# Three score rounds of the second batch put into one burst of a planned attention and feed-forward kernel

## The chip, the cores and the metric

The kernel runs on one core of a Trainium2 chip. The metric is the time of one execution in device microseconds (us); several executions are timed and the median is given. One execution was also recorded by the hardware profiler. Its engines are called PE (TensorE, matmuls), PEld (TensorE's weight loads), DVE (VectorE), ACT (ScalarE), POOL (GpSimd) and SP (SyncE, which here only issues transfers).

## The reference

Eight batches of twelve heads, with 448 positions and 64 elements per head. The attention has a squared ReLU in the place of a softmax, and its output goes straight into a feed-forward block with the same squared ReLU.

```
scores = scale * q @ k.T                  # per batch and head, 448 x 448
attn   = max(scores, 0) ** 2 / S          # S = 448
x      = (attn @ v), heads side by side   # 3584 x 768
g      = max(x @ w_in, 0) ** 2            # 3584 x 2048
out    = g @ w_out                        # 3584 x 768, float32
```

## The kernel before, in words

**Units and rounds.** A unit is four heads of one batch, so there are three units to a batch and 24 in all. The 448 positions are cut into seven blocks of 64. A round is one unit and one key block: `scores` (L525) multiplies four heads at once on TensorE as four 64x64 tiles, four matmuls that fill two PSUM banks. Rounds are numbered through: 0 to 20 belong to the first batch, 21 to 41 to the second. `squared` then empties each bank twice: `rel` = ReLU of the bank by DVE (L541) or ACT (L544), and `at` = its square by ACT (L548) or POOL (L551). When the seven rounds of a unit are squared, `av` (L591) multiplies them with v (28 matmuls in 64x64 tiles), and ACT or DVE (L611, L613) copies the result into `xt`.

**Dense work.** With a batch's `xt` complete, 16 groups of six matmuls (L653) make `g`; ACT squares the bank (L642) and DVE masks it (L637). The second product is done by a Strassen scheme: seven products of eight matmuls (L873) in place of eight. Its sums of `g` are made by DVE (`comb`, L852), its combinations of `w_out` also by DVE (`wt`, L839), and its results are put together by ACT and DVE (L793, L795, L885) and stored by SP (L749).

**Loads.** Units 0 to 5 of q and k are turned on TensorE (L463) and copied out by ACT or DVE (L466); from unit 6 on POOL casts them (L443) and SP issues a transposing transfer (L479). POOL issues the loads of v (L492), of the early q and k (L409), of `w_in` (L499) and of `w_out` (L504). The first batch is a special stream (L702, L715, L729, L732 make the first columns of `g`; L1023 are filler matmuls that the plan puts where TensorE would be idle early on).

**What sets the order.** Nothing is issued as it is written. Every operation is added to a `Plan` with a cost, its dependencies, its buffers and a due time; for matmul groups the due time is a running sum of their costs, `plan.now`. `Plan.run` then plays the plan through with sixteen pairs of rules (how long TensorE stays idle before a filler, and when POOL may take a square) and up to ten guesses of when loads land, keeps the pair whose end is earliest, and emits the instructions in the order of their planned starts. Which engine takes a `rel` or a square, which buffer is used, and the order on every queue come out of this.

**Bursts.** From the second batch on, `bursts()` gives groups of rounds. For each group the loop at L1122 adds the loads and turns that are due by then, adds the scores of its rounds, links them (`glue`: TensorE prefers the next linked piece, and waits up to 0.45 us of plan time for it), puts the `av` of the finished unit behind the second round where the group names one, and then calls `run_some`, which adds dense work in proportion to the length of the group. The first groups are listed by hand in `FIRST` (L1000); later units have groups of four and three rounds.

Of the kernel before, what the change touches and what calls it, by code (L numbers as in the profile page):

```python
# [300 lines left out]
def kernel(  # L301
# [654 lines left out]
    def push_dense(b):  # L956
# [36 lines left out]
        if b == 0 and PLAIN0:  # L993
# [3 lines left out]
    EARLY = 6  # L997
    PLAIN0 = False
    NPE = 6
    FIRST = (((21,), None), ((22, 23), None), ((24, 25), None), ((26, 27), None), ((28, 29), None),  # L1000
             (range(30, 34), 3), ((34, 35), None), ((36, 37), None), (range(38, 42), 4))
    STEPS = (0, 1, 2, 3), (4, 5, 6)
    ROUNDS = NUN * TJ
# [2 lines left out]
    def bursts():  # L1006

        for rs, n in FIRST:
            yield list(rs), n
# [187 lines left out]
```

## Time and profile before

| | |
|---|---|
| median of 6 runs | 379.53 us (378.63 to 380.4) |
| the profiled execution | 378.72 us, of which the span is 376.9 us |
| granted TensorE clock in it | 0.999 |
| PE busy | 366.5 us, 3277 matmuls |
| DVE, ACT, POOL busy | 272.7, 269.3, 221.0 us |
| moved by DMA | 51.36 MB |

The span runs from the first to the last recorded instruction; 1.82 us of the execution lie outside it. Busy times of PE and PEld overlap. A releaser in the profile is what ended an engine's idle time, and the chain is followed back from the last instruction to whatever released each step.

### The profile page before, as it was taken

What the parts mean: (1) busy time and instruction counts of PE and PEld (TensorE: products, weight loads), DVE (VectorE), ACT (ScalarE), POOL (GpSimd) and SP (SyncE); (2) the same over time, 40 slices, a digit from 0 to 9 for tenths busy, and PEclk for the clock granted to TensorE, in tenths of its full rate; (3) what the DMA queues carried; (4) which work ended last, traced back from release to release, by engine and by line L of the source; (5) the groups of instructions that cost most, each with busy time, mean ns of one, the idle gap of its engine ahead of it and who ended that gap; (6) DMA issues with size and microseconds to landing.
All of it is one profiled execution on the core that took longest, in us unless ns stands there. A gap on an engine that the chain in (4) does not pass through costs nothing.

```text
span 376.9 us, 8786 instructions
## 1 busy us (share of the span) xinstructions
PE 366.5 (97%) x3277; PEld 196.6 (52%) x3277; DVE 272.7 (72%) x472; ACT 269.3 (71%) x587; POOL 221.0 (59%) x271
## 2 busy tenths in 40 slices
PE   7799999999999999999999999999999999999995
PEld 3446555444455445545555555545555555555663
DVE  2996899968967777677977666868777687366631
ACT  5998998869966898688767678677777675243221
POOL 7999975768766777566486567856575333000100
PEclk9999999999999999999999999999999999999999
DMA  8999998497598683971588873774643002210243
GB/s 180 197 208 203 204 232 227 134 170 241 120 197 205 179 183 58 220 164 26 149 135 197 199 173 72 190 167 92 152 81 92 3 12 52 55 30 0 64 104 84
DMA packets 70218, 51.36 MB, mean 136 GB/s; under 512 B 36896, under 2 KB 70176, under 8 KB 70176
## 3 DMA queue, kind: packets, MB, share of 16 engines
q1 hardware_dynamic: 52384, 35.86, 37.9%
q0 software_dynamic: 16928, 14.09, 25.2%
q10 hardware_dynamic: 864, 0.85, 0.7%
q8 instruction: 25, 0.41, 0.4%
q14 instruction: 17, 0.14, 0.1%
HBM read 45.61 MB, written 11.01 MB: 150 GB/s over the span
## 4 chain that ended last, share of the span: by engine, by line
PE 90%; POOL 3%; ACT 2%; DMA 2%; DVE 1%; issue 1%; ACTq 0%; POOLq 0%; DVEq 0%
PE mm L653 38%; PE mm L873 34%; PE mm L525 9%; PE mm L591 8%; DMA g<-in_k_dram 2%; ACT at L548 1%; POOL w L499 1%; POOL comb L551 1%; PE mm L463 1%; DVE rel L541 1%; PE mm L702 1%; POOL vs L492 1%; ACT rel L544 0%; ACT part L793 0%; POOL g L409 0%
## 5 line engine op out<-in xcount | busy, mean ns | idle before, releaser
L551 POOL TENSOR_TENSOR at<-rel 128x448 f16<-128x448 f32 (+1 forms) x148 | 133.9, 928 | 69.1 <-DVE rel L541 51.4
L653 PE MATMUL mm<-xt,w 128*128 128x448 f16 (+1 forms) x768 | 147.8, 346 | 0.0
L637 DVE SCALAR_TENSOR_TENSOR g<-mm,g 128x448 f16<-128x448 f32 (+1 forms) x128 | 77.0, 605 | 46.4 <-ACT g L642 46.1
L653 PEld LDWEIGHTS <-w 128*128 128x128 f16 x768 | 73.1, 98 | 67.9 <-issue 7.4
L642 ACT ACTIVATE g<-mm 128x448 f16<-128x448 f32 (+1 forms) x128 | 69.6, 545 | 49.7 <-PE mm L653 49.4
L541 DVE TENSOR_SCALAR rel<-mm 128x448 f32<-128x448 f32 (+3 forms) x172 | 95.0, 594 | 11.8 <-PE mm L525 10.4
L548 ACT ACTIVATE at<-rel 128x448 f16<-128x448 f32 (+1 forms) x188 | 98.9, 593 | 0.3 <-DVE rel L541 0.3
L544 ACT ACTIVATE rel<-mm 128x448 f32<-128x448 f32 (+2 forms) x176 | 84.9, 557 | 4.6 <-PE mm L525 4.6
L873 PEld LDWEIGHTS <-comb 128*128 128x128 f16 x448 | 42.1, 98 | 33.4 <-issue 5.9
L525 PE MATMUL mm<-qkt,qkt 64*64 64x448 f16 (+2 forms) x756 | 49.6, 336 | 0.9 <-DVE rel L541 0.4
L885 DVE SCALAR_TENSOR_TENSOR part<-mm,part 128x384 f32<-128x384 f32 x56 | 30.5, 554 | 24.8 <-ACT part L793 13.3
L793 ACT ACTIVATE part<-mm 128x384 f32<-128x384 f32 x42 | 21.1, 505 | 35.4 <-PE mm L873 34.6
L443 POOL CAST blk<-raw 128x896 f16<-128x896 f32 x36 | 33.3, 930 | 20.2 <-DVE wt L839 6.5
L873 PE MATMUL mm<-w,comb 128*128 128x384 f16 x224 | 39.8, 327 | 0.0
L873 PE MATMUL mm<-wt,comb 128*128 128x384 f16 x224 | 39.6, 326 | 0.0
L873 PEld LDWEIGHTS <-g 128*128 128x128 f16 x288 | 27.7, 98 | 20.6 <-issue 2.5
L591 PE MATMUL mm<-at,vs 64*64 64x448 f16 (+1 forms) x672 | 35.2, 343 | 0.2
L873 PE MATMUL mm<-w,g 128*128 128x384 f16 x192 | 33.9, 326 | 0.3 <-DVE rel L541 0.3
L525 PEld LDWEIGHTS <-qkt 64*64 64x64 f16 x756 | 18.9, 105 | 24.2 <-issue 19.1
L492 POOL DMA_DIRECT2D vs<-in_v_dram x48 | 29.9, 632 | 1.8 <-DMA g<-in_k_dram 1.1
L774 POOL COPY rest<-g 128x1024 f16<-128x1024 f16 x8 | 8.4, 1050 | 36.0 <-DVE comb L852 35.3
L591 PEld LDWEIGHTS <-vs 64*64 64x64 f16 x756 | 21.5, 107 | 14.9 <-issue 3.8
(59 smaller groups left out, 197.2 us busy)
## 6 DMA issues: line engine op xcount, KB each, us to landing
out_dram<-part SPq DMA_DIRECT2D x108, 96.0 KB, 2.3
raw<-in_k_dram SPq DMA_DIRECT2D x18, 448.0 KB, 4.3
raw<-in_q_dram SPq DMA_DIRECT2D x18, 448.0 KB, 5.5
vs<-in_v_dram POOLq DMA_DIRECT2D x48, 112.0 KB, 5.1
w<-in_moe_w_in_dram POOLq DMA_DIRECT2D x4, 768.0 KB, 12.1
w<-in_moe_w_out_dram POOLq DMA_DIRECT2D x4, 768.0 KB, 13.5
g<-in_k_dram POOLq DMA_DIRECT2D x4, 224.0 KB, 10.8
g<-in_q_dram POOLq DMA_DIRECT2D x4, 224.0 KB, 9.8
```

Of the source, the lines that this page charges most:

```text
L443: return lambda: fn(blk.tile.rearrange("p t (f d) -> p f t d", f=2), tile_of().rearrange("p f (t d) -> p f t d", d=D))
L492: return lambda: nc.gpsimd.dma_start(out=buf.tile[64 * r:64 * r + 64], in_=src[:, u, hs])
L525: nc.tensor.matmul(sp[e].tile[64 * c:64 * c + 64, c0:c0 + w].rearrange("p (t c) -> p t c", c=TP), lhsT=kT[r, t, 64 * e:64 * e + 64], rhs=q ...
L541: dve(width, lambda: nc.vector.tensor_scalar(out=r.tile[:, 0:width], in0=bank.tile[:, 0:width], scalar1=0.0, scalar2=SK, op0=ALU.max, op1= ...
L544: act(width, lambda: nc.scalar.activation(out=r.tile[:, 0:width], in_=bank.tile[:, 0:width], func=AF.Relu, scale=SK))],
L548: act(width, lambda: nc.scalar.activation(out=dst(), in_=r.tile[:, 0:width], func=AF.Square)),
L551: lambda: nc.gpsimd.tensor_mul(dst(), r.tile[:, 0:width], r.tile[:, 0:width]))],
L591: nc.tensor.matmul(banks[f].tile[64 * e:64 * e + 64, c0:c0 + w], lhsT=vs[r, e ^ c, t * D:(t + 1) * D], rhs=a[r, e, :], start=(t == 0), sto ...
L637: nc.vector.scalar_tensor_tensor(out=dst, in0=src, scalar=0.0, in1=dst, op0=ALU.is_gt, op1=ALU.mult)
L642: nc.scalar.activation(out=dst, in_=src, func=AF.Square)
L653: nc.tensor.matmul(bank.tile[:, c0:c0 + w], lhsT=w1[f // 4][:, m, f % 4 * P:(f % 4 + 1) * P], rhs=xts[b].tile[:, m, cols], start=(m == 0), ...
L873: nc.tensor.matmul(buf.tile[:, 0:HALF], lhsT=lhs()[:, j, :], rhs=w[:, j, :], start=(first and j == 0), stop=(j == NH - 1), skip_group_chec ...
```

## The change

The first two entries of the hand-written list become one. Rounds 21, 22 and 23 are now one group, linked and followed by one call of `run_some`; before, round 21 was a group with a call of its own, and rounds 22 and 23 were the next group. Everything else in the program text is the same, but the plan is made anew, and the built program differs on every engine from its first microseconds on.

```
     EARLY = 6
     PLAIN0 = False
     NPE = 6
-    FIRST = (((21,), None), ((22, 23), None), ((24, 25), None), ((26, 27), None), ((28, 29), None),
+    FIRST = (((21, 22, 23), None), ((24, 25), None), ((26, 27), None), ((28, 29), None),
              (range(30, 34), 3), ((34, 35), None), ((36, 37), None), (range(38, 42), 4))
```

More of the change, by code (lines that the diff above doesn't have):

```diff
@@ L999 @@
     NPE = 6
-    FIRST = (((21,), None), ((22, 23), None), ((24, 25), None), ((26, 27), None), ((28, 29), None),
+    FIRST = (((21, 22, 23), None), ((24, 25), None), ((26, 27), None), ((28, 29), None),
              (range(30, 34), 3), ((34, 35), None), ((36, 37), None), (range(38, 42), 4))
```

## The prediction

> **What bounds the kernel now.** I read the page first, then the busy time by stretch, the chain of waits in order of time, TensorE's own waits, and TensorE's timeline where the edit lies. A change of 0.3%, 1.14 us, is about the least that a measurement of this kernel can tell from none.
>
> The page, TensorE's row and its 40 slices:
>
> ```profile
> PE 366.5 (97%) x3277; PEld 196.6 (52%) x3277; DVE 272.7 (72%) x472; ACT 269.3 (71%) x587; POOL 221.0 (59%) x271
> ...
> PE   7799999999999999999999999999999999999995
> ```
>
> The busy time by stretch (PE, PEld, DVE, ACT, POOL, then clock, DMA share, GB/s):
>
> ```profile
> 20.00:30.60 10.60, 9.80 (x128) 5.29 (x127) 9.61 (x23) 10.60 (x29) 10.54 (x16) 1.00 1.24 206
> 30.60:36.00 5.40, 5.40 (x96) 3.46 (x94) 2.68 (x5) 4.19 (x10) 5.40 (x9) 1.00 1.27 205
> 36.00:60.00 24.00, 24.00 (x286) 14.16 (x284) 22.30 (x42) 23.88 (x57) 20.98 (x27) 1.00 1.20 220
> 60.00:100.00 40.00, 39.66 (x334) 19.44 (x332) 34.40 (x57) 34.01 (x76) 28.52 (x34) 1.00 0.80 173
> 100.00:372.00 272.00, 271.88 (x2148) 145.48 (x2147) 190.85 (x320) 181.12 (x387) 137.51 (x159) 1.00 0.51 116
> ```
>
> Until 30.6 ACT and POOL are full and TensorE has holes; afterwards TensorE is full, with hardly a hole to the end. TensorE's waits from 36 us on are this one line:
>
> ```profile
> PE mm L873 <- DVE rel L541: 0.3, 1, 0.3
> ```
>
> TensorE's timeline around the edited rounds (21 to 23 are the 12 matmuls at 35.99):
>
> ```profile
> 29.79 0.99 PE L1023 MATMUL mm<-part 128*128 128x256 f16 x5
> 30.62 1.46 PE L702 MATMUL mm<-w,xt 128*128 128x512 f16 x6
> 32.01 0.58 PE L463 MATMUL mm<-ident,g 128*64 128x128 f16 x14
> 32.52 1.15 PE L591 MATMUL mm<-at,vs 64*64 64x320 f16 x28
> 33.60 0.58 PE L463 MATMUL mm<-ident,g 128*64 128x128 f16 x14
> 34.11 0.62 PE L729 MATMUL mm<-ident,comb 128*128 128x128 f16 x8
> 34.57 0.98 PE L653 MATMUL mm<-xt,w 128*128 128x320 f16 x6
> 35.48 0.58 PE L463 MATMUL mm<-ident,g 128*64 128x128 f16 x14
> 35.99 0.76 PE L525 MATMUL mm<-qkt,qkt 64*64 64x448 f16 x12
> ```
>
> The chain, for the price of a switch between 64x64 tiles and dense matmuls:
>
> ```profile
> 231.09 1.32 PE mm L591 x28
> 232.41 0.38 PE mm L525 x8
> 232.79 1.41 PE mm L873 x8
> 234.20 1.14 PE mm L653 x6
> ...
> 240.03 2.27 PE mm L653 x12
> 242.30 1.30 PE mm L873 x8
> 243.60 0.50 PE mm L525 x8
> ```
>
> Eight score matmuls take 0.38 us behind other tiled ones and 0.50 behind dense ones; eight of L873 take 1.30 behind dense and 1.41 behind tiled ones. A switch costs 0.12 into tiles and 0.11 out.
>
> The sum of before, from the burst at 36.06 to TensorE's end at 372.75 (336.7 us): 672 dense matmuls of 448 columns at 0.189 (127.0), 90 of 320 columns at 0.136 (12.2), 784 of L873 at 0.1625 (127.4), 588 of L525 and 588 of L591 at 0.0473 (27.8 each), 42 turns at 0.036 (1.5): 323.7. With 102 switches (11.7) that is 335.4; 1.3 us is left for all waits. Nothing much can be won behind 36 us; a loss has no such bound.
>
> **The change part by part.** At its own place the edit does nothing: the trace already has the 12 matmuls of the three rounds in one stretch. What changes is what the planner makes of it. I compared the built orders engine by engine.
>
> *Up to 30.6 us.* The four L702 groups start at 19.15, 23.09, 27.05 and 30.62, and the `w_in` parts landed at 19.1, 23.0, 26.7 and 30.5 (issue plus time to landing): the stage is paced by these landings, 3.7 to 3.9 us apart, whenever they were issued. POOL now issues the last three behind a 320-column square (0.70) in place of a 512-column one (1.06), 0.36 earlier. I take 0; the bounds are -0.36 (each landing follows its issue) and +0.3 (ACT's work to its fourth L715 is 29.1 us by its rows, 28.8 before, and ACT is full there). Two switches more lie here, under the landings.
>
> *30.6 to 37 us.* Before, L591 stood between unit 3's two turns. Now both turns come first, and the second needs its q, issued at 16.5 and landed at 32.8, while TensorE is ready at 32.5: +0.25, bounds 0 and 0.6. The burst then comes before an L653 and a turn that preceded it: 1.33 us of work exchanged, no cost. Unit 4's loads are issued up to 0.7 later; q landed at 36.2 and is needed at about 37: hidden, and 0.2 if that cover goes.
>
> *Switches.* From the burst on there are 98 in place of 102: -4 x 0.11 = -0.44. Over the whole kernel it is 116 for 118, so the bounds are -0.22 and -0.44.
>
> *Bank waits.* In the old order one PSUM bank is reused 0.5 us after its last write (the L873 at 98.97, the wait of 0.34 above). The new order spaces that one out, but in the burst near 73 us an L653 follows the 12 matmuls into the bank that their first pair filled, also 0.5 us after. ACT's `rel` (0.48) with about 0.2 to start it frees it 0.2 to 0.3 late: -0.34 + 0.3.
>
> *The `w_out` loads (L504).* POOL has 0.68 us more ahead of the first, and a 448-column square (0.93) between the first two. They landed at 44.7, 48.5, 52.3 and 58.6. DVE's first L839 stands five rows earlier, at about 50.4, and needs the second: 50.1 at the latest. Every `rel` behind it on DVE's queue, and so TensorE's banks, would wait with it. The fourth is needed by L873 at 59.7 and comes at 60.2 at the latest: +0.1, bounds 0 and 0.5.
>
> *Squares on POOL.* POOL takes 159 in place of 151 over the kernel: 8 x 0.93 = 7.4 us, under 156 us of its idle time; ACT has 8 fewer. I take 0; without that cover each costs its 0.93.
> By the Trainium skill ("SBUF — State Buffer", "SBUF: two separate sides") GpSimd and a VectorE operation with two SBUF inputs hold a shared port in turn, the loser blocked for the whole instruction, which speaks against more squares on POOL. The trace agrees: the first `wt` on DVE took 1.69 us beside a square, others 0.945. By that rule 8 squares could add 8 x 0.74 = 6 us to DVE, beside 104 us of its idle time, and the sum stays what it is.
>
> *Unit 7's transposes.* POOL casts k behind four squares now, not ahead of them; SP issues the two L479 back to back behind four stores; and TensorE wants the pair before its next L591 (1.45 us), not behind it. By adding up the rows the second L479 is issued near 75.7; time to landing ran from 2.9 to 7.1, so it lands between 78.6 and 82.8. TensorE needs it near 81.9 (83.3 before, when it landed at 79.4). I take 0.2, nearest to the 4.9 that the last one took; bounds 0 and 0.9.
>
> Sum: 0 + 0.25 - 0.44 - 0.34 + 0.3 + 0.1 + 0 + 0.2 = +0.07. On the profiled execution that is 378.72 + 0.07 = 378.8; the median of the runs stands 0.81 above it: 379.6. With all low bounds the sum is -1.1, with all high ones +2.2.
>
> **The rivals.** *Unit 7 arrives late (slower).* The mechanism above, with POOL one cast and one square further behind (1.85): a landing at 83 to 84.7 against 81.9 stops TensorE for 1 to 2.8 us, and no later stage has slack to give back. It decides from a landing behind 83. For it: 6.0 and 7.1 us are the landings of the pair issued at 77.9 and 79.3. Against it: the pair before took 2.9 and 4.9. Time: 379.4 (the forecast without its 0.2 for this) + 1.9, the middle, = 381.3.
>
> *ACT and DVE fall behind between 36 and 60 us (slower).* ACT has 0.12 us idle of 24 there, and DVE now runs both halves of its first L839 (1.25 to 1.69 each) before 58 us, where the second stood at 59.2. If one half lands in front of a `rel` for which TensorE has no other bank, TensorE waits that long, less the 0.2 or so in which a bank is not yet wanted: 379.6 + 1.3 = 380.9. Against it: the counts of `rel`, mask and L839 in that stretch are the same in both orders.
>
> *The early landings move (faster).* If the landings follow their issue, -0.36, the switches give -0.44, and the bank wait goes without another in its place, -0.34, and the exchange of turns costs nothing: -1.1 to -1.3, 378.3. For it: POOL is on the chain there. Against it: the even 3.8 us between landings.
>
> *The change doesn't do what it says.* At the place it names that holds already; had the planner made the same order, the time would be 379.5. The built orders differ, so this goes with the forecast.
>
> **How the numbers follow.** Forecast, within 1.1 us: 0.46. Unit 7 late: 0.22. ACT and DVE behind: 0.14. Early landings: 0.18. Slower by over 0.3%: most of the two slow cases (0.31) and the forecast's upper edge (0.07): 0.38. Faster: 0.18 and its lower edge 0.04: 0.22. Within: 0.40. The forecast's own range is 378.5 to 380.7; to hold 8 in 10 it goes to 378.2, into the fast case, and to 382.2, the late unit with 2.8 us.
>
> **What would show it.** Right: L702 at the same four times within 0.3; about 0.25 us before the second turn near 32.8; one short bank wait near 73 and none near 99; TensorE's chain unbroken from 37 us to the end. Wrong: a TensorE wait over 0.5 on a DMA near 82 or on DVE or ACT between 45 and 60; or the fourth L702 moved from 30.6 by more than 0.4.

## The result, and the profile after

The changed kernel takes 381.17 us in the median (21 runs, 379.43 to 382.47); the kernel before takes 379.16 us on the same chip (47 runs). The ratio is 1.0046, with a 95% interval of 1.0035 to 1.0057: slower by 1.3 to 2.2 us (the quotient of the two medians is 1.0053, inside the interval). The profiled execution took 380.41 us with a span of 378.6 (before 378.72 and 376.9), at a granted clock of 1.00. The profile of the first experiment below comes from a disturbed execution, so only that run's times are used.

The page of the changed kernel, TensorE's row and its 40 slices:

```profile
PE 369.0 (97%) x3277; PEld 197.9 (52%) x3277; DVE 271.0 (72%) x469; ACT 268.4 (71%) x582; POOL 226.2 (60%) x279
...
PE   8889999999999999999999999999999999999995
```

TensorE is still the bound, with the same 3277 matmuls, so the 1.7 us must be holes, later starts or matmuls that take longer (PE is busy 2.5 us more, 1.4 of it before 20 us: 16.43 against 15.06). Its waits from 33 us on hardly show them:

```profile
PE mm L653 <- ACT rel L544: 0.2, 1, 0.2
PE mm L525 <- DVE g L637: 0.2, 1, 0.2
```

These two stand in place of the one wait of 0.3 before. The rest is found by laying the two timelines beside each other at the same work. First TensorE's timeline of the changed kernel around the edited rounds:

```profile
31.16 1.47 PE L702 MATMUL mm<-w,xt 128*128 128x512 f16 x6
32.56 0.58 PE L463 MATMUL mm<-ident,g 128*64 128x128 f16 x14
33.07 0.28 PE L1023 MATMUL mm<-part 128*128 128x256 f16 x1
33.45 0.58 PE L463 MATMUL mm<-ident,g 128*64 128x128 f16 x14
33.96 1.15 PE L591 MATMUL mm<-at,vs 64*64 64x320 f16 x28
35.04 0.62 PE L729 MATMUL mm<-ident,comb 128*128 128x128 f16 x8
35.59 0.76 PE L525 MATMUL mm<-qkt,qkt 64*64 64x448 f16 x12
```

The fourth L702 starts at 31.16, 0.54 later than before. The filler at 33.07 covers a hole of 0.38 ahead of unit 3's second turn, whose q was issued at 16.3 and landed at 33.4. The L591 that stood at 47.18 stands at 48.10 (+0.92), so more than half of the loss is made by then. The score burst that stood at 113.37 begins at 114.36 (+0.99). The last step is near 217 us, in the chain of waits:

```profile
215.80 0.64 DVE g L637
216.44 0.02 issue
216.46 1.29 DVE comb L852
217.75 1.07 DVE rel L541 x2
218.83 0.04 issue
218.87 0.38 PE mm L525 x2
```

DVE's sum for the Strassen product (`comb`) took 1.29 us in place of 0.70, because a cast on POOL ran beside it (216.28 to 217.21):

```profile
216.28 0.93 POOL L443 CAST blk<-raw 128x896 f16<-128x896 f32 x1 [0.22 <-DMA raw<-in_q_dram]
```

That the cast is the reason is shown by the second profile of the same program, below. The two `rel` behind it freed TensorE's banks late, and the L873 that follows came 1.58 after its old place in place of 0.99. From there both timelines keep that distance to the end (374.34 against 372.75).

### The profile page after: what moved, and what is told of

Read it like the earlier page. It is cut to its first block, busy times and chain, and to the rows that moved or that the text cites. A ratio compares the mean times of both kernels' runs of the same rounds, so it can differ in the third digit from the quotient of the medians.

```text
span 378.6 us, 8785 instructions
## 1 busy us (share of the span) xinstructions
PE 369.0 (97%) x3277; PEld 197.9 (52%) x3277; DVE 271.0 (72%) x469; ACT 268.4 (71%) x582; POOL 226.2 (60%) x279
## 4 chain that ended last, share of the span: by engine, by line
PE 86%; DMA 6%; ACT 2%; POOL 2%; DVE 2%; issue 1%; ACTq 0%; POOLq 0%
PE mm L653 36%; PE mm L873 33%; PE mm L525 8%; PE mm L591 7%; DMA g<-in_q_dram 5%; DMA g<-in_k_dram 2%; POOL w L499 1%; ACT rel L544 1%; PE mm L463 1%; ACT at L548 1%; POOL comb L551 1%; ACT g L642 1%; DVE g L637 1%; DVE rel L541 0%; DVE part L885 0%
## 5 line engine op out<-in xcount | busy, mean ns | idle before, releaser
L551 POOL TENSOR_TENSOR at<-rel 128x448 f16<-128x448 f32 (+1 forms) x156 | 139.6, 918 | 71.0 <-DVE rel L541 44.1
L541 DVE TENSOR_SCALAR rel<-mm 128x448 f32<-128x448 f32 (+2 forms) x166 | 92.7, 596 | 15.8 <-PE mm L525 14.0
L548 ACT ACTIVATE at<-rel 128x448 f16<-128x448 f32 (+1 forms) x180 | 93.2, 586 | 0.8 <-DVE rel L541 0.8
L544 ACT ACTIVATE rel<-mm 128x448 f32<-128x448 f32 (+2 forms) x182 | 86.7, 546 | 6.7 <-PE mm L525 6.5
L873 PEld LDWEIGHTS <-comb 128*128 128x128 f16 x448 | 42.3, 98 | 33.1 <-issue 5.4
L525 PE MATMUL mm<-qkt,qkt 64*64 64x448 f16 (+2 forms) x756 | 50.7, 336 | 1.5 <-ACT xt L611 0.6
L885 DVE SCALAR_TENSOR_TENSOR part<-mm,part 128x384 f32<-128x384 f32 x56 | 30.5, 554 | 25.6 <-ACT part L793 15.0
L793 ACT ACTIVATE part<-mm 128x384 f32<-128x384 f32 x39 | 19.3, 495 | 36.5 <-PE mm L873 36.4
L873 PE MATMUL mm<-w,comb 128*128 128x384 f16 x224 | 39.8, 327 | 0.0
L873 PE MATMUL mm<-wt,comb 128*128 128x384 f16 x224 | 39.6, 326 | 0.0
L873 PEld LDWEIGHTS <-g 128*128 128x128 f16 x288 | 27.5, 98 | 20.9 <-issue 2.9
L591 PE MATMUL mm<-at,vs 64*64 64x448 f16 (+1 forms) x672 | 35.2, 343 | 0.1
L873 PE MATMUL mm<-w,g 128*128 128x384 f16 x192 | 34.0, 326 | 0.0
L525 PEld LDWEIGHTS <-qkt 64*64 64x64 f16 x756 | 18.7, 105 | 26.0 <-issue 20.1
L591 PEld LDWEIGHTS <-vs 64*64 64x64 f16 x756 | 21.7, 107 | 13.5 <-issue 3.1
```

Source lines behind the costliest of these rows:

```text
L525: nc.tensor.matmul(sp[e].tile[64 * c:64 * c + 64, c0:c0 + w].rearrange("p (t c) -> p t c", c=TP), lhsT=kT[r, t, 64 * e:64 * e + 64], rhs=q ...
L541: dve(width, lambda: nc.vector.tensor_scalar(out=r.tile[:, 0:width], in0=bank.tile[:, 0:width], scalar1=0.0, scalar2=SK, op0=ALU.max, op1= ...
L544: act(width, lambda: nc.scalar.activation(out=r.tile[:, 0:width], in_=bank.tile[:, 0:width], func=AF.Relu, scale=SK))],
L548: act(width, lambda: nc.scalar.activation(out=dst(), in_=r.tile[:, 0:width], func=AF.Square)),
L551: lambda: nc.gpsimd.tensor_mul(dst(), r.tile[:, 0:width], r.tile[:, 0:width]))],
L591: nc.tensor.matmul(banks[f].tile[64 * e:64 * e + 64, c0:c0 + w], lhsT=vs[r, e ^ c, t * D:(t + 1) * D], rhs=a[r, e, :], start=(t == 0), sto ...
```

## The experiments

All times are medians; each ratio is against the kernel before, run beside it on the same chip (379.0 to 379.4 us). Differences of 0.1% between two of these runs are within their intervals.

My first theory was that the planner's other pair of rules made the loss. The pair is (patience, lead): how long TensorE stays idle before a filler, and how far ahead of ACT POOL must be to take a square. The planner chose (0.45, 0.9) for the kernel before and (0.3, 1.1) for the changed one.

The end that `Plan.run` works out when a kernel is built says what the planner itself expected: 378.8 us of plan time for the old list with (0.45, 0.9), and 378.5 for the new list with (0.3, 1.1). The old list with (0.3, 1.1) comes to 380.0 and the new list with (0.45, 0.9) to 380.9. So the planner took the changed kernel for 0.3 us faster, and the first two experiments build plans that it had turned down as 1.3 and 2.1 us slower than the old one; their loss does not by itself explain that of the changed kernel.

**The new list with the rules of before.**

```
-    PATIENCE = 0.0, 0.15, 0.3, 0.45
-    LEAD = 0.7, 0.9, 1.1, 1.3
+    PATIENCE = 0.45,
+    LEAD = 0.9,
```

> The new list, with the planner held to the pair of rules that it picked for the old list (idle 0.45 us before a filler, lead 0.9; it had picked 0.3 and 1.1). The built order is that of the kernel before on every engine up to about 37 us. Theory S (the start costs: in the profiles the new kernel is 0.92 us late at the first L591 behind 36 us, 48.27 against 47.35): that L591 comes back to 47.4 within 0.3, and the ratio to before falls from 1.0046 to 1.002 or less. Rival P (the loss is the DVE and POOL collision near 217 us and others like it behind 48 us): L591 may move but the ratio stays at 1.003 or more. Rival N (the early difference is the luck of one profile): the landings of w_in differ from run to run by 0.5 whatever the order.

380.40 us, ratio 1.0043 (1.0028 to 1.0058). The rules of before do not bring the time back. Whether the L591 came back is not seen here; a later run with the same plan has it at 47.21, as before.

**The old list with the new rules** (0.3 and 1.1 put there in the same way).

> The old list, with the planner held to the pair of rules that it picked for the new one (0.3 and 1.1). The built order is that of the changed kernel up to about 33 us (up to the second turn of unit 3 and the L591 on TensorE). Theory S: the four L702 start 0.4 to 0.8 later than before (19.15, 23.09, 27.05, 30.62), the first L591 behind 36 us is 0.5 to 0.9 late, and the time is 1.002 to 1.003 of before at least. Rival P: the ratio depends on what comes behind 48 us alone. Rival N: L702 at the times of before within 0.2.

380.88 us, ratio 1.0046 (1.0029 to 1.0064). Its start is the changed kernel's, with the wait of 0.48 before the first L702 and the L591 at 47.79. But the four L702 (19.79, 23.14, 26.81 and 30.80) are not 0.4 to 0.8 late as expected: the last is 0.18 behind the kernel before. Behind that TensorE waits 0.4, 0.3 and 0.3 for banks, near 90, 100 and 183 us, where the kernel before waits 0.3 once. So the old list loses as much under the new rules as the new list does under either pair; 1.3 of its 1.6 us the planner had expected.

**Unit 3's second turn behind the L591 again.** After the planning, the turn of q is moved in the emitted order to where it was before; `tags` finds operations by a name given to them.

```
+ turn, late = tags["turn", 3, "q"], tags["av", 2, 128]
+ # the turn and its copy go directly behind `late`
```

> The changed kernel with one move on TensorE: the second turn of unit 3 (L463, q) goes behind the L591 of unit 2, where it stood before; all else is emitted as in the changed kernel. Theory S: the 0.37 us between 33.07 and 33.45, in which TensorE waits for q to land, goes, and everything behind it comes 0.3 to 0.4 us earlier: ratio 1.0036 against 1.0046. Rival: q lands while ACT and DVE are what the burst waits for (its copies of the turn end later now), and less than 0.15 comes back.

380.33 us, ratio 1.0032 (1.0011 to 1.0052). The hole went, but the copy of the turn (L466 on ACT) then came late for the burst, which waited 0.45 at 35.61; at 48.12 nothing was gained: from the fourth L702 (30.83) it took 17.3, where the changed kernel took 16.9. The time can't tell this run from the changed kernel. This profile showed something else, a wait in TensorE's row that the changed kernel's first profile does not have:

```profile
94.93 0.57 PE L525 MATMUL mm<-qkt,qkt 64*64 64x448 f16 x8 [1.84 <-DMA qkt<-blk]
```

**The changed kernel a second time**, without any edit.

> The changed kernel once more, for a second profile of the same order. Theory S and the account of the first profile: L702 near 19.98, 23.57, 27.39 and 31.16 again, 0.9 us late against before at 48 us, and L873 behind the two score rounds near 219 us late by another 0.6, since POOL's cast is beside DVE's comb there. Rival N: one or both are gone, at the same median.

380.76 us, ratio 1.0026 (1.0001 to 1.0052). The twelve executions run from 378.80 to 383.03, and three of them (378.80, 378.82, 378.83) lie below the median of the kernel before, 379.26. So an execution of the changed order can go without most of the loss; none of these three was profiled. In the profiled one (381.36) the four L702 stand at 20.11, 23.91, 27.67 and 31.47, and the L591 at 48.44. The same wait is there, at 94.53:

```profile
PE mm L525 <- DMA qkt<-blk: 1.1, 1, 1.1
PE mm L653 <- ACT rel L544: 0.2, 1, 0.2
```

It is unit 8's second transposing transfer. SP's queue in the changed kernel's first profile (start, time to issue; the last line merges unit 8's second transpose with the next one of the queue):

```profile
79.62 0.59 SPq L392 DMA_DIRECT2D raw<-in_k_dram  x1
80.32 1.25 SPq L479 DMA_TRANSPOSE qkt<-blk  x1
81.61 0.66 SPq L392 DMA_DIRECT2D raw<-in_q_dram  x1
82.39 8.09 SPq L479 DMA_TRANSPOSE qkt<-blk  x2
```

Two loads of 448 KB for unit 9 now stand ahead of and between unit 8's two L479; before, both L479 came first:

```profile
77.89 2.64 SPq L479 DMA_TRANSPOSE qkt<-blk  x2
80.58 0.58 SPq L392 DMA_DIRECT2D raw<-in_k_dram  x1
81.22 0.65 SPq L392 DMA_DIRECT2D raw<-in_q_dram  x1
```

The second L479 took 10.7 us to land in the first profile (at 93.1, just as TensorE needed it), 11.5 in this one and 12.3 in the run above; before it took 7.0 and landed at 86.3. Near 217 us the sum and the cast met the other way round:

```profile
217.73 0.69 DVE L852 TENSOR_TENSOR comb<-g 128x1024 f16<-128x1024 f16 x1
217.86 1.35 POOL L443 CAST blk<-raw 128x896 f16<-128x896 f32 x1 [0.20 <-DMA raw<-in_q_dram]
```

Here the sum kept its 0.69 and the cast took 1.35 in place of 0.93. From the score burst to the L873 behind it TensorE took 2.32 (217.52 to 219.84), as in the kernel before (2.33), where the first profile shows 2.93. So the 0.6 there is the price of this meeting, and the losses behind 50 us change from one execution to the next.

**Unit 9's two loads behind unit 8's two transposes.**

```
+ # the loads of raw ("raw", 9, "k") and ("raw", 9, "q") go behind
+ late = tags["flip", 8, "q"]      # unit 8's second L479
```

> The changed kernel; only SP's two loads of unit 9 (L392, raw) are moved from ahead of and between unit 8's two transposes (L479) to behind both. Theory (the raw loads delay unit 8's second transpose, and TensorE waits for it near 94 us): it is issued about 0.6 earlier, near 81.8, lands in 5 to 8 us instead of 10.7 to 12.3, so at 87 to 90, and TensorE's L525 near 94 waits for nothing on a DMA; the time falls by 0.2 to 1.8, most likely by 0.9, to about 380.0. Rival A (the loss is all in the first 50 us and in chance): the transposes come early but the time stays within 0.3 of the changed kernel, near 380.9. Rival B (the loads then come late themselves): unit 9's cast and transpose move back by over 2 us and TensorE waits near 107 instead; no gain.

380.84 us, ratio 1.0039 (1.0025 to 1.0052). The mechanism is as expected: the transpose was issued at 82.0, took 5.8 and landed at 87.8, and the wait on it is gone. The time is that of the first rival (near 380.9). It did not fall, and the trace shows where it went. DVE and POOL:

```profile
90.05 0.93 POOL L443 CAST blk<-raw 128x896 f16<-128x896 f32 x1 [2.27 <-DVE g L637]
...
100.47 0.92 POOL L443 CAST blk<-raw 128x896 f16<-128x896 f32 x1
```

```profile
100.34 1.60 DVE L852 TENSOR_TENSOR comb<-g 128x1024 f16<-128x1024 f16 x1
```

Unit 9's k, issued at 83.25 in place of 79.62, landed 6.6 later, at 89.9, and its cast on POOL moved from 88.30 to 90.05. All POOL work behind it moved by the same 1.7, which brought a cast to 100.47, 0.13 behind the start of a `comb` on DVE. That one then took 1.60 in place of 0.68, and TensorE's next product came 0.6 later. Another 0.5 went at 75 us for a reason that the edit has no part in: DVE's L885 waited until 74.10 for the buffer that a store (L749, issued at 65.9) frees, and this store took 8.1 us to land (at 74.0) where the first profile shows 6.4. The trace names an L873 as the releaser there; that it was the store is read from the times.

**The kernel before with the new order of these four transfers.** Only the two L479 are moved, each behind one load.

> The kernel before; only unit 8's two transposes (L479) are moved on SP's queue, the first behind the load of unit 9's k and the second behind the load of its q, which is the order that the changed kernel has there. Theory (the raw loads delay the transposes): the second one is issued near 80 instead of 79.3 and takes 9 to 12 us instead of 7.1, landing at 89 to 92.5 against a need at 93.3: little or no wait, time 379.2 to 379.8 against 379.3; the landing is the number that counts. Rival A (time to landing does not depend on the loads ahead): it lands at 87 to 88 and nothing changes. Rival B (the delay adds up to the whole loss): TensorE waits 1 us or more on it near 93 and the time is 380.3 or more.

379.32 us, ratio 1.0002 (0.9991 to 1.0014). The second L479, issued at 81.0, took 8.8 and landed at 89.8; TensorE needed it at 93.5. So the order of the queue costs the landing 2.3 us against the second profile of before (79.5 + 8.0 = 87.5; 1.5 of it is the later issue) and 3.5 against the first, which the old order has to spare.

**The kernel before a second time**, without any edit.

> The kernel before, unchanged, for a second profile of it. If the changed kernel's later start (first score burst behind 36 us 0.9 later) is the order's doing, the four L702 stand again at 19.1, 23.1, 27.1 and 30.6 within 0.3, and unit 8's second transpose lands near 86 with 7 us to spare. If it is the spread of the landings, the fourth L702 is anywhere between 30.6 and 31.5. Ratio 1.000 within 0.002.

379.30 us, ratio 1.0002 (0.9990 to 1.0013). L702 at 19.36, 23.29, 27.27 and 30.85; from the L591 at 47.40 to the end 329.8 us, against 329.7 in the first profile. In these two profiles the old order repeats to 0.1 us behind its start.

**The new list, the rules of before, unit 9's loads behind** (the first edit and the one on the loads together).

> The changed kernel with the planner held to the pair of rules that it chose for the kernel before (patience 0.45, lead 0.9), as in the first run of this study, and with unit 9's two loads moved on SP's queue behind unit 8's two transposes, as in the run with the loads behind. Theory (what the first run lost, 1.1 to 1.6 us, is the same wait): no TensorE wait on a DMA near 94, time 379.2 to 379.9. Rival (its loss is in the order of TensorE and of the squares behind 44 us): the time stays at 380.2 to 380.6 with the transposes early.

380.43 us, ratio 1.0034 (1.0020 to 1.0048): the rival. Its start is that of before (fourth L702 at 30.65, L591 at 47.21) and no transfer holds TensorE behind it, but TensorE waits for banks:

```profile
PE mm L525 <- DVE g L637: 0.5, 1, 0.5
PE mm L653 <- ACT rel L544: 0.4, 1, 0.4
PE mm L525 <- ACT rel L544: 0.3, 1, 0.3
PE mm L873 <- ACT rel L544: 0.3, 1, 0.3
```

That is 1.5 in place of 0.3, and from the L591 to the end it takes 331.4 in place of 329.8. In this plan bank waits are 1.2 of the 1.6 us lost; the start is not late and no transfer is.

**The loads of `w_in` closer together, in the kernel before.** The last three L499 go directly behind the first, ahead of a POOL square.

> The kernel before; only the last three loads of w_in (L499) are moved on POOL's queue from behind a 512-column square to directly behind the first, so they are issued about 1.06 earlier, near 11.0 in place of 12.1. It is the changed kernel's move (0.36 earlier) made larger. Theory (parts issued closer together share the transfers and the first of them lands later): the four L702 start later than at 19.1, 23.1, 27.0 and 30.7, the first by 0.5 or more and the fourth by 0.3 to 0.8, and the time rises by as much, to 379.6 to 380.1. Rival A, which the prediction named (the landings follow their issue): the fourth L702 near 29.7, time 378.3. Rival B (the stage is paced by the bytes, whatever the issue): the four within 0.2 of before, time 379.3.

380.91 us, ratio 1.0040 (1.0024 to 1.0055), but not for the reason expected. The square that they passed came 3.1 us later, TensorE waited for it (1.73 <- POOL `comb` L551 at 15.42), and everything moved by 2.2; the fourth L702, at 32.83, was behind its landing. So TensorE does not show the landings here, but the trace has them: issued 0.4 earlier than in the kernel before (11.8 to 13.5), the three parts landed at 23.0, 26.9 and 31.3, against 22.9, 26.7 and 30.5. Earlier issue gave no earlier landing. The run also shows that POOL's squares bound the start as closely as the landings do.

**The loads of `w_in` further apart, in the changed kernel.** The three L499 go behind one more square.

> The changed kernel; only the last three loads of w_in (L499) are moved on POOL's queue behind one more square (512 columns, 1.06), so they are issued near 13.1 in place of 12.1 and further from the first. Theory (close issue makes them land later): the first L702 comes earlier than at 20.0, at 19.0 to 19.3, the fourth at 30.6 to 30.9 in place of 31.2 to 31.5, and the time falls by 0.3 to 0.6 against the changed kernel, to about 380.4. Rival A (the landings follow their issue): all four up to 1.0 later, the fourth near 32, time 381.8. Rival B (the changed kernel's later start has another reason): the fourth stays at 31.0 to 31.5 and the time at 380.8.

383.06 us, ratio 1.0098 (1.0076 to 1.0121). The square that they were put behind waited 2.39 us for ACT, so they were issued at 15.34 in place of 12.05, and the L702 came at 22.22 to 35.01. Issued 3.3 later than in the changed kernel, the three parts landed at 24.5, 28.3 and 32.1, in place of 23.6, 27.3 and 31.1: only 0.9 to 1.0 later. Both runs speak against landings that follow their issue. Since squares moved too, neither says why the last part lands later in the new order.

**The new list, the rules of before for 36 us and the new ones from then on.**

```
             now = heapq.heappop(events)
+            self.patience, self.lead = (0.45, 0.9) if now < 36.0 else (0.3, 1.1)
```

> The changed kernel, but the planner is held to the pair of rules of the kernel before (0.45, 0.9) for the first 36 us of plan time and to those that it chose for the changed kernel (0.3, 1.1) from then on. The built order is that of the kernel before up to about 54 us on TensorE, and a new one behind it. Theory (0.9 of the loss of 1.7 comes from the start order, the rest from places behind it where a transfer or a bank is just late): the first score burst behind the L591 near 47.2 stands as before, and the time is 379.5 to 380.3. Rival (the loss is made by the list of bursts itself, behind 60 us): the start is as before and the time still 380.7 or more.

381.41 us, ratio 1.0058 (1.0041 to 1.0075): the rival. TensorE's order is that of before up to about 54 us and the L591 stands at 47.58, but behind it lie five waits, 0.7 on a `w_out` load and 0.4, 0.4, 0.3 and 0.2 on banks. A good start does not bring a good rest. The planner's own end for this plan is 380.9, so it expected a loss here too.

**Three places of the changed kernel at once.** The first two stores go ahead of the two loads in front of them; unit 9's loads go behind unit 8's transposes; POOL's two loads of unit 3's v go behind the next 320-column square.

> The changed kernel with three orders on the queues changed, each seen in its own place of the trace. One: SP's two loads ahead of the first two stores (near 65 us) go behind them. Two: unit 9's two loads go behind unit 8's two transposes, as in the run with the loads behind. Three: POOL's two loads of unit 3's v (near 17.4 us) go behind its next 320-column square. Theory (the loss of the changed kernel is small lateness at these places): the stores land in 2 to 4 us, by 68, in place of 6.4 to 8.5, and DVE's L885 near 73 is not held; unit 8's second transpose lands by 90 and TensorE's L525 near 94 has no wait on a DMA; the first L702 loses its wait of 0.5 on DVE and starts near 19.6 in place of 20.0. What then remains is the fourth L702 near 31.0, the wait before unit 3's second turn and chance meetings of POOL's casts with DVE's sums: time 379.9 to 380.4, against 380.8 to 381.2 for the changed kernel. Rival (each wait that goes is replaced by the next one, as in the two runs that moved a single step): the places are mended and the time stays at 380.7 or more.

380.58 us, ratio 1.0037 (1.0022 to 1.0052): between the theory's 380.4 and the rival's 380.7, and not to be told from the changed kernel. The profiled execution was one of the slowest (382.34). In it the places are as expected: the stores landed in 4.4 us, the transpose at 89.0 (82.1 + 6.9), the first L702 at 19.36. But other losses stood in their place: the wait of 0.49 on DVE now stands before the second L702 (23.83), and at 99.92 us a `comb` took 2.28 beside POOL's squares and cast:

```profile
PE mm L873 <- DVE comb L852: 0.9, 2, 0.7
```

## Why the prediction was right in its range, and where its steps failed

The time, 381.17, is within the range, 1.6 above the forecast, on the side that had 0.38. It lies close to the first rival's 381.3, but that rival did not happen as written. The sum failed: it forecast +0.07, and the change costs 1.3 to 2.2 us. (The forecast stood on 379.53, the median of six runs, where 47 runs give 379.16.) The range reached up to 382.2 for a late unit 7, which was not late; that the time lies inside is luck as far as the steps go. Three steps failed: two terms put at 0 (the start-up, and POOL's work, which met DVE's sum), and the transposes of unit 8, which no term covers. The sign "chain unbroken from 37 us" failed too, at 215.2. Point by point:

*Start-up (0, bounds -0.36 and +0.3): the largest miss.* The four L702 came 0.83, 0.48, 0.34 and 0.54 late, the last beyond the 0.4 that was to prove the step wrong. I took the landings as the only pace. In DVE's row of the changed kernel:

```profile
19.43 0.92 DVE L541 TENSOR_SCALAR rel<-mm 128x320 f32<-128x320 f32 x2 [0.89 <-POOL at L551]
```

POOL now has a 128-column square ahead of its loads of v, so its next square starts at 18.66 in place of 18.41; DVE waits for the `rel` buffer that this square frees, and the first L702 waits 0.48 for the bank. This wait is in all five profiles with this start order (0.48 to 0.54) and in none with the old one. But the landings were later too: the last part of `w_in` took 17.4 to land where it took 16.6, issued no later. Counted from the issue of the first part, the last landed after 20.4 to 20.9 us in these five profiles and after 20.2 to 20.7 in five of the old order. The fourth L702 stood at 30.80 to 31.47 in these five (mean 31.11), and at 30.62 to 31.01 in the five with the old order (mean 30.76). About 0.35 in the mean goes with the order, though the ranges overlap, and the rest of the 0.54 with the single execution. Why the landings come later is open. That I gave the landings no gain from their earlier issue was right: the two runs on it show landings that hardly follow the issue.

*Second turn (+0.25, bounds 0 and 0.6): right, mis-sized.* It measured 0.38 (33.07 to 33.45). From the fourth L702 to the L591 near 48 us it takes 16.9 to 17.0 in four profiles of the new order against 16.6 in five of the old one.

*Switches (-0.44) and bank waits (-0.34 + 0.3): the waits right, the gain not found.* The wait near 99 is gone and one of 0.21 stands at 74.81, as forecast; one of 0.19 at 93.26 is extra. But from 48 to 114 us, where the four fewer switches lie, the changed kernel lost 0.07. Waits account for 0.06 of the 0.5 that is missing; an L525 that took 0.73 in place of 0.56 and the burst at 73.74 that took 0.86 in place of 0.76 for 0.27 more. The rest is open.

*`w_out` loads (+0.1): nothing*; no such wait in the trace.

*Squares on POOL (0): right in the small.* Behind 33 us no wait of TensorE is put down to them. What I left out is POOL's casts and squares meeting DVE's `comb`. The row that I had weighed, 1.69 against 0.945 for a `wt`, was the price of such a meeting; its place was not looked for. By the Trainium skill ("SBUF — State Buffer", "SBUF: two separate sides") the operation that starts second is blocked for the whole of the other. The runs show the blocking, but not from the recorded starts which one is blocked: of two sums that began 0.13 ahead of a cast, one took 1.60, which is its own 0.68 and the cast's 0.92, and the other kept its 0.69 while the cast took 1.35.

*Unit 7's transposes (+0.2), and the first rival: the right mechanism at the wrong unit.* Unit 7's second L479 took 4.1 and landed at 81.2, against a need at 82.85, where the L525 shows no wait. Unit 8's pair, which I used only as a measure of how long a landing can take, was itself pushed behind loads and cost 0 to 1.8 us. The order was in the built program; I followed the queue one unit too short.

*The chain.* I said that little could be won behind 36 us and that a loss has no such bound. The three other plans (the new list with the rules of before, the old list with the new rules, the rules by time; ratios 1.0043, 1.0046 and 1.0058) are each slower than the order before by 1.1 to 2.4 us, and the waits differ from plan to plan. They are weak support, since the planner itself put them 1.3 to 2.1 us behind it.

So this is shown: the edit makes the planner lay out everything anew; it took the new layout for 0.3 us faster, and in its two profiles it is 1.7 and 2.4 us slower by the span, through lateness that its plan does not foresee. About 0.9 us of the first profile's 1.7 is the start under the new rules, 0.6 the meeting of a cast and a sum near 217 us, and in other executions 1.1 to 1.8 is unit 8's transpose. The old layout has only 0.3 us of waits behind 33 us, in both of its profiles; why it is spared the rest is not shown. That these swings explain why the median stands 0.8 above the profiled execution is likely, not shown.

## What to carry to other kernels

Where one engine is full and a planner places everything, an edit of the list is a new draw of the whole layout: judge it by every wait that the new order could have, not by the place of the edit, and not by the planner's own end, which was 0.3 us lower for the slower kernel here. Follow each queue for the units behind the one that you look at, and write down for each transfer its landing and its need; the one with the least to spare decides, and its landing depends on what stands ahead of it. Removing one wait only helps if the next resource has room: here a load moved by 3.6 us came back as a cast that met another engine's sum 17 us later. Lay a loss of half a per cent to a place only when a second profile of the same program shows it too.

## What the runs showed of the hardware that was not expected

The time to landing of one and the same transposing transfer, the second of unit 8, ran from 4.7 to 8.0 us in six profiles with no load ahead of or between the pair, and from 8.7 to 12.3 in five with a 448 KB load ahead of each. A 96 KB store with two 448 KB loads directly ahead of it took 5.9 to 8.9 us to land, and 4.4 with the loads behind it. The last parts of `w_in`, issued 3.3 us later, landed 0.9 to 1.0 later. DVE's sum of two SBUF tiles took 0.68 alone and 1.29, 1.60 and 2.28 beside POOL; in another execution POOL's cast paid instead (1.35 in place of 0.93).
